# Moving the second product half a unit later and reordering ScalarE's work in a fused top-k attention and gated feed-forward kernel

## The chip, the cores and the metric

The kernel runs on one core of one Trainium2 chip. The metric is device time in microseconds (us) of that core. A core has five engines that are programmed separately: TensorE (PE in the profile, with its weight loads as PEld), VectorE (DVE), ScalarE (ACT), GpSimd (POOL) and SyncE (SP), which here only issues transfers. Each engine works through its own queue of instructions in order and waits on semaphores for the others.

## The reference

There are two blocks in a row. Attention with 8 batches, 8 heads, 576 positions and a head size of 64 keeps the 32 largest scores of each row. Its output, 4608 tokens of 512 values, goes through a feed-forward block whose activation is h cos(h).

```python
scores = scale * np.matmul(q, k.transpose(0, 1, 3, 2))
kth = np.partition(scores, -32, axis=-1)[..., -32:-31]
scores = np.where(scores >= kth, scores, -1000000000.0)
attn = np.exp(scores - np.max(scores, axis=-1, keepdims=True))
attn = attn / (np.sum(attn, axis=-1, keepdims=True) + 1e-09)
x = np.matmul(attn, v)          # then (B,H,S,D) -> (B*S, H*D)
h = x @ w_in                    # 512 -> 2048
out = (h * np.cos(h)) @ w_out   # 2048 -> 512
```

All of it is in float32.

## The kernel before

**Units, blocks and slots.** A unit is one pair of heads for 128 tokens; there are 144. Four units make a block of 128 tokens, of which there are 36. Since 576 is four and a half times 128, every ninth block straddles two batches, and its units have two parts. The main loop makes one pass a unit, called a slot here. In slot i several units are in work at once: unit i (called u) has its 32 largest values searched, the unit before (w) is masked and exponentiated, older ones (x, y, z) are normalised, transposed and multiplied by the values.

**Attention.** `scores` (L213) puts a unit's scores into a PSUM tile `sc` and a shared bank `rim`, and `take_scores` (L228) copies them to `s` on ScalarE. `topk_first` and `topk_round` search on VectorE, which takes most of that engine's time; the middle units are first folded in two halves (`fold`, L235, line 244), and the folded search of w is closed by two small reductions (`merge_first`, `merge_second`, L289 and L296) at the start of the next slot. On ScalarE `bounds` (L309) makes the threshold and the maximum from the merged result, `mask` (L322) pushes everything below the threshold far down, and `exponentials` (L330) makes the weights and their sum `den`. In the next slot VectorE's `reciprocal` (L341, line 343) is the first instruction, so its start marks the start of a slot on that engine. GpSimd's `normalise`, `split` and a transfer then write the weights out in two half-words, a transposing transfer (`transposes`, L367) brings them back as `pT`, and every second slot `values` (L391) multiplies two units at once and `take_values` (L410) copies the result to `xT`.

**The feed-forward block.** It is fed into gaps of the attention. `ff1` (L450) is an eighth of a block's first product, with two eighths to a PSUM bank `mm`; `ff2` (L533) is an eighth of the second product, and all eight of a block add up in one bank `o`. These banks come from the same pool of two. A full bank is put on the list `full`. `take_banks` (L482) empties the listed banks on ScalarE, with `take_first` (`take_g` in the text, L477) for an mm bank and `take_second` (`take_o`, L551) for an o bank. The activation is made for half a block at a time: `reduce_first` and `reduce_second` on GpSimd bring the argument into range, `sines` (L516) runs on ScalarE, and `gate` (L526) multiplies on GpSimd. Sine and exponential need different function tables on ScalarE, so a table load stands where they alternate.

**What sets the order.** The order on each engine is written out by hand: each queue gets its instructions in the order in which `slot` (L666) emits them. Slots 9 to 140 use `slot`; the early and the late ones have functions of their own. `feed(n)` (L575) emits up to n pieces of the feed-forward block. It raises a counter `tick`, spends credit (each slot adds 5 less 0.9 for every unit whose scores it makes, up to 5.3), and takes two pieces of one kind and then two of the other, as far as `can_first` (L560) and `can_second` (L568) allow. `can_second` holds an ff2 back until its gate lies at least two ticks behind. Credit that no piece may use is lost above the cap. A loop at the end of the kernel, the drain, emits two pieces a pass until nothing is left.

In a block that lies in one batch, odd slots make the scores of two units (`made` has two entries) and even slots make none. In a straddling block each slot makes the scores of one unit. Odd slots also run `values` (z is set).

Of the kernel before, what the change touches and what calls it, by code (L numbers as in the profile page):

```python
# [31 lines left out]
def kernel(  # L32
# [16 lines left out]
    NP = H // 2  # L49
# [46 lines left out]
    ff = {"live": 0, "tick": 0, "now": 0, "credit": 0.0, "end": False, "kind": 0, "half": 0, "open": 0}  # L96
# [34 lines left out]
    def decode_second(n):  # L131


        for _ in range(min(n, len(wq["second"]))):
            st, w = wq["second"].popleft()
            wi = w.bitcast(I32)
            nc.vector.tensor_scalar(out=w, in0=w, scalar1=2.0, scalar2=None, op0=ALU.max)
            nc.vector.tensor_scalar(  # L138
                out=wi, in0=wi, scalar1=3, scalar2=None, op0=ALU.logical_shift_left
            )  # L140
            wq["third"].append((st, w))
# [24 lines left out]
    NU = len(units)  # L166
    pairs = {}
    v_tails = []
    for i in range(2 * NP):
        t = consts.tile([P, P], F32, tag=f"v_tail{i}", name=f"v_tail{i}")  # L170
# [79 lines left out]
    for i in range(3):  # L250
        t = consts.tile([P, 2, TOPK, 2], F32, tag=f"top{i}", name=f"top{i}")
# [5 lines left out]
    def topk_first(u, w):  # L257

        u["top"] = tops[u["n"] % len(tops)]
        merges = [merge_first, merge_second] if w and w["folds"] else []  # L260
        if u["folds"]:
            for op in (ALU.max, ALU.min):
                fold(u, op)
                if merges:
                    merges.pop(0)(w)
        else:
            u["rest"] = work.tile([P, 2, S], F32, tag="rest", name="rest", bufs=1)
        for merge in merges:
            merge(w)
        topk_round(u, 0)  # L270

    def topk_round(u, rnd):
        top, rest, lasts = u["top"], u["rest"], TOPK // 8 - 1
        end = TOPK - 1 - 8 * rnd
        at = top[:, :, end : end - 8 if rnd < lasts else None : -1, 0]
        if u["folds"]:
            search(at, rest[:, :, 0:HS], rest[:, :, 0:HS], rnd < lasts)
            if rnd < TOPK // 16:

                low = top[:, :, 1 + 8 * rnd : 9 + 8 * rnd, 1]  # L280
                search(low, rest[:, :, HS:S], rest[:, :, HS:S], rnd < TOPK // 16 - 1)
        else:
            search(at, u["s"] if rnd == 0 else rest, rest, rnd < lasts)
        if rnd == lasts:
            del u["rest"]
# [36 lines left out]
    def mask(u):  # L322

        s, nb = u["s"], u.pop("nb")
        for j in range(2):
            nc.scalar.activation(  # L326
                out=s[:, j], in_=s[:, j], func=AF.Prelu, bias=nb[:, j, 1:2], scale=SCALE, alpha=FAR
            )
# [12 lines left out]
    def reciprocal(u):  # L341
        u["rden"] = small.tile([P, 2], F32, tag="rden", name="rden")
        nc.vector.reciprocal(u["rden"], u.pop("den"))  # L343
# [47 lines left out]
    def values(us):  # L391


        o = room[0]
        for i, u in enumerate(us):
            pT = u.pop("pT")
            for b, _, rows, r0 in u["parts"]:
                st = pairs[b, u["hp"]]
                r = slice(r0, r0 + rows)
                to = slice(i * P + r0, i * P + r0 + rows)  # L400
                for c in range(NT + 1):
                    for j in range(2):
                        d = slice(j * D, (j + 1) * D)
                        if c < NT:
                            lhsT, rhs = st["v"][:, c, d], pT[:, j * (NT + 1) + c, r]
                        else:
                            lhsT, rhs = st["v_tail"][:, d], pT[:, NT, r]
                        nc.tensor.matmul(o[d, to], lhsT, rhs, start=c == 0, stop=c == NT)  # L408
# [16 lines left out]
    for w in widths:  # L425
        blk = {"t0": t0, "w": w, "left": 0, "g": [], "gated": []}
# [23 lines left out]
    def ff1(blk, i):  # L450
        w = blk["w"]
        nf = 256 // w
        part = i % 4
        if part == 0:
            blk["g"].append(ffw.tile([P, 1024], F32, tag="g", name="g", bufs=CHUNKS))
            ff["live"] += 1
        if part % 2 == 0:
            open_bank()
            blk["mm"] = ps.tile([P, 512], F32, tag="mm", name="mm", bufs=2)
        g, mm = blk["g"][-1], blk["mm"]  # L460
        for a in range(nf):
            f = i * nf + a
            at = (part % 2 * nf + a) * w
            for c in range(NC):
                nc.tensor.matmul(  # L465
                    mm[:, at : at + w],
                    w_in[f // FC][:, c, (f % FC) * P : (f % FC + 1) * P],
                    blk["xT"][:, c],
                    start=c == 0,
                    stop=c == NC - 1,  # L470
                )
        if part % 2 == 0:
            return
        ff["open"] -= 1
        full.append((take_first, blk, g, mm, part // 2))
# [6 lines left out]
    def take_banks():  # L482
        while full:
            take, *what = full.popleft()
            take(*what)
# [40 lines left out]
    def gate(n):  # L526
        for _ in range(min(n, len(sined))):
            blk, g, x = sined.popleft()
            eng = nc.vector if ff["end"] else nc.gpsimd
            eng.tensor_tensor(out=g, in0=g, in1=x, op=ALU.mult)  # L530
            blk["gated"].append(ff["tick"])

    def ff2(blk, i, f0):  # L533
        w = blk["w"]
        if f0 == 0:
            open_bank()
            blk["o"] = ps.tile([P, 512], F32, tag="mm", name="o2", bufs=2)
        o = blk["o"]
        per = 1024 // w
        for f in range(f0, f0 + 2):  # L540
            g = blk["g"][f // per]
            at = (f % per) * w + i * P
            nc.tensor.matmul(  # L543
                o, g[:, at : at + P], w_out[f], start=f == 0, stop=f == NF - 1
            )
        if f0 + 2 < NF:
            return
        ff["open"] -= 1
        full.append((take_second, blk, i, o))
# [18 lines left out]
    def can_second():  # L568
        if not second:
            return False  # L570
        blk, i, f = second[0]
        gated = sum(ff["tick"] >= t + 2 for t in blk["gated"])
        return gated * 1024 // blk["w"] >= f + 2 and wq["ready"] >= NC * NF // FC + f + 2

    def feed(n):  # L575

        ff["tick"] += 1
        while n > 0 and ff["credit"] >= 1:
            for kind in (ff["kind"], 1 - ff["kind"]):
                if (can_first, can_second)[kind]():  # L580
                    break
            else:
                return
            if kind == 0:
                ff1(*first.popleft())
            else:
                ff2(*second.popleft())
            if kind != ff["kind"] or ff["half"]:
                ff["kind"], ff["half"] = 1 - kind, 0
            else:  # L590
                ff["half"] = 1
            n, ff["credit"] = n - 1, ff["credit"] - 1
# [73 lines left out]
    def slot(i, u, w, x, y, z):  # L666
        if x:
            reciprocal(x)
        if u:
            topk_first(u, w)  # L670
            decode_second(2)
        if u:
            topk_round(u, 1)
            topk_round(u, 2)
            topk_round(u, 3)
        if z:
            values(z)
        made = scored.get(i, [])
        if not made or not z:
            feed(1)  # L680
        for m in made:
            scores(m)


        late = z and len(made) == 2
        if not made:
            take_banks()
        if w:
            bounds(w)
            mask(w)  # L690
        if w and late:
            exponentials(w)
        take_banks()
        if z:
            take_values(z)
        take_scores(units[i + 1])
        if w and not late:
            exponentials(w)
        for load, b, hp in at_slot.get(i, []):
            load(b, hp)  # L700
        load_weights(2)
        if y:
            transposes(y)
        gate(1)
        if x:
            normalise(x)
            split(x)
            write_halves(x)
        feed(2)
        take_banks()  # L710
        decode_third()
        decode_first(2)
        reduce_first()
        reduce_second()
        feed(1 if late else 3)
        if i % 2:
            sines(1)
        elif i < EARLY + 8 or i > LAST - 2:
            sines(2)
# [51 lines left out]
    for i in range(NU + 1):  # L771
# [6 lines left out]
        z = units[i - 5 : i - 3] if i % 2 and EARLY <= i - 5 < LAST else None  # L778
# [53 lines left out]
```

## Time and profile before

The time is 1538.96 us, the median of three runs (1538.32 to 1544.69); the profiled execution spans 1537.8 us.

| engine | busy us | share of the span |
|---|---|---|
| TensorE, matmuls | 1419.5 | 92% |
| TensorE, weight loads (beside the matmuls) | 1018.8 | 66% |
| VectorE | 1416.3 | 92% |
| ScalarE | 1158.8 | 75% |
| GpSimd | 1105.3 | 72% |

The chain of work that ended last is TensorE for 80% of the span; line 465 (first product) and line 543 (second product) make 30% each, line 408 (values) 10%, line 220 (scores) 9%. The costliest groups are VectorE's search for maxima (L304, 681.6 us), the first product (L465, 554.5 us of matmuls), the second product (L543, 529.4 us) and VectorE's replacing of found maxima (L307, 495.0 us). The granted clock of TensorE is 1.00 in most of the span, lower in the first 250 us and at some places later.

In the views below, a wait is the time for which an engine stood still before an instruction, and the name after the arrow is what ended it. Idle time of an engine that is not the bound costs nothing, so a wait counts only where the engine that waits is short of time.

### The profile page before, as it was taken

Reading aid. Unit: us, or ns where it says so; the run is one execution under the profiler, and the core shown is the slowest. Engines: PE = TensorE matmul, PEld = TensorE weight load, DVE = VectorE, ACT = ScalarE, POOL = GpSimd, SP = SyncE. Lnnn points to the kernel's source line nnn. Section 1 sums busy time; section 2 is a strip of 40 time slices with the busy share of each in tenths; the row PEclk is TensorE's granted clock in tenths of the full one; section 3 lists DMA queues with packets and bytes.
Section 4 is the critical chain, followed back from the end, with each engine's and each line's share of the span. In section 5 each row is a group of like instructions: output and inputs, shape, how many; then the busy total and the mean of one; then the engine's idle time right before and its main releaser. Section 6 shows DMA issues by size and latency. Waiting matters only on the chain.

```text
span 1537.8 us, 30197 instructions
## 1 busy us (share of the span) xinstructions
PE 1419.5 (92%) x10360; PEld 1018.8 (66%) x10360; DVE 1416.3 (92%) x4689; ACT 1158.8 (75%) x2326; POOL 1105.3 (72%) x838
## 2 busy tenths in 40 slices
PE   4577789999999999999999999999999999999999
PEld 2365366777677766777777766777777766777675
DVE  7989998999999998999999998999999998999821
ACT  7888776777777777777777777777777776777741
POOL 4777966777777776777777776777777776777610
PEclk6687899999999999999999999999999999999999
DMA  8422465545654456545564455545555455545300
GB/s 270 139 85 71 113 192 132 145 133 169 162 147 132 132 155 164 163 131 148 167 162 137 133 146 162 158 130 154 170 163 129 133 136 143 133 130 132 99 8 14
DMA packets 371753, 212.20 MB, mean 138 GB/s; under 512 B 321296, under 2 KB 337936, under 8 KB 371600
## 3 DMA queue, kind: packets, MB, share of 16 engines
q1 hardware_dynamic: 366192, 200.63, 47.3%
q10 hardware_dynamic: 5408, 9.65, 1.8%
q8 instruction: 81, 1.33, 0.4%
q14 instruction: 72, 0.59, 0.1%
HBM read 45.09 MB, written 87.29 MB: 86 GB/s over the span
## 4 chain that ended last, share of the span: by engine, by line
PE 80%; ACT 8%; DVE 4%; POOL 3%; DMA 2%; SPq 1%; issue 1%; ACTq 0%; POOLq 0%; DVEq 0%
PE mm L465 30%; PE o L543 30%; PE rim L408 10%; PE sc L220 7%; PE rim L220 2%; ACT g L478 2%; DVE top L304 2%; ACT s L334 1%; DVE rest L307 1%; DMA pT<-rows 1%; ACT s L326 1%; DVE w_out L138 1%; POOL s L348 1%; ACT st L127 1%; ACT s L230 1%
## 5 line engine op out<-in xcount | busy, mean ns | idle before, releaser
L304 DVE MAX8 top<-rest 128x8 f32<-128x288 f32 (+1 forms) x1656 | 681.6, 460 | 0.0
L465 PEld LDWEIGHTS mm<-xT,w_in 128*128 128x128 f32 x4608 | 538.3, 194 | 80.1 <-ACT g L478 41.0
L465 PE MATMUL mm<-xT,w_in 128*128 128x128 f32 x4608 | 554.5, 279 | 32.8 <-ACT g L478 32.8
L543 PE MATMUL o<-w_out,g 128*128 128x512 f32 x1152 | 529.4, 602 | 12.7 <-POOL g L530 6.8
L307 DVE MATCH_REPLACE8 rest<-top,rest 128x288 f32<-128x288 f32 (+1 forms) x1104 | 495.0, 456 | 0.0
L543 PEld LDWEIGHTS o<-w_out,g 128*128 128x128 f32 x1152 | 209.5, 192 | 228.9 <-issue 208.8
L360 POOL COPY halves<-s 128x2304 uint16<-128x2304 uint16 x132 | 277.7, 2103 | 17.1 <-DMA rows<-halves 9.2
L348 POOL TENSOR_SCALAR s<-s,rden 128x576 f32<-128x576 f32 x288 | 212.8, 751 | 52.1 <-DVE rden L343 52.1
L530 POOL TENSOR_TENSOR g<-g,x 128x1024 f32<-128x1024 f32 x68 | 160.6, 2362 | 99.3 <-ACT x L523 86.8
L334 ACT ACTIVATE s<-s,nd 128x576 f32<-128x576 f32 x288 | 220.0, 765 | 0.8
L244 DVE TENSOR_TENSOR rest<-sc,s 128x576 f32<-128x576 f32 x264 | 198.6, 753 | 8.0 <-ACT s L231 2.3
L326 ACT ACTIVATE s<-s,nb 128x576 f32<-128x576 f32 x288 | 205.4, 760 | 0.0
L504 POOL TENSOR_SCALAR x<-g 128x1024 f32<-128x1024 f32 x68 | 71.1, 1046 | 168.7 <-ACT g L478 168.7
L408 PEld LDWEIGHTS rim<-pT,v 128*64 128x64 f32 x2560 | 134.8, 141 | 71.6 <-ACT g L478 23.5
L408 PE MATMUL rim<-pT,v 128*64 128x128 f32 (+1 forms) x2560 | 162.9, 272 | 15.7 <-ACT pT L389 13.3
L478 ACT ACTIVATE g<-mm 128x512 f32<-128x512 f32 x144 | 84.5, 588 | 122.3 <-PE mm L465 122.3
L513 POOL TENSOR_TENSOR x<-g,x 128x1024 f32<-128x1024 f32 x68 | 161.1, 2370 | 5.7
L220 PE MATMUL sc<-k,q 64*128 64x448 f32 (+1 forms) x640 | 150.7, 585 | 14.9 <-DMA k<-in_k_dram 8.9
L314 ACT ACTIVATE nb<-top 128x4 f32<-128x4 f32 x144 | 29.4, 204 | 141.2 <-DVE top L297 129.0
L230 ACT COPY s<-sc 128x896 f32<-128x896 f32 x144 | 128.9, 895 | 6.6 <-PE sc L220 6.2
L220 PEld LDWEIGHTS rim<-k,q 64*128 64x128 f32 (+1 forms) x640 | 57.2, 182 | 58.9 <-issue 53.9
L523 ACT ACT_TABLE_LOAD x68 | 87.2, 1283 | 1.6 <-ACT ob L553 0.4
(55 smaller groups left out, 1244.1 us busy)
## 6 DMA issues: line engine op xcount, KB each, us to landing
rows<-halves SPq DMA_DIRECT2D x132, 576.0 KB, 2.9
out_dram<-ob ACTq DMA_DIRECT2D x36, 256.0 KB, 3.4
q<-in_q_dram SPq DMA_DIRECT2D x31, 288.0 KB, 3.2
st<-in_moe_w_in_dram SPq DMA_DIRECT2D x16, 512.0 KB, 5.5
v<-in_v_dram SPq DMA_DIRECT2D x32, 256.0 KB, 3.2
st<-in_moe_w_out_dram SPq DMA_DIRECT2D x16, 512.0 KB, 3.5
k<-in_k_dram SPq DMA_DIRECT2D x31, 144.0 KB, 3.3
k<-in_k_dram SPq DMA_DIRECT2D x32, 128.0 KB, 3.5
```

What stands on the lines that cost most here:

```text
L220: nc.tensor.matmul(to[r0 : r0 + rows, j, 0 : k1 - k0], st["q"][d, q0 : q0 + rows], st["k"][d, k0:k1], start=True, stop=True,)
L244: nc.vector.tensor_tensor(out=u["rest"][:, :, i * HS : (i + 1) * HS], in0=sc[:, :, 0:HS], in1=s[:, :, HS:S], op=op,)
L304: nc.vector.max(to[:, j], src[:, j])
L307: nc.vector.match_replace(rest[:, j], to[:, j], src[:, j], NEG)
L326: nc.scalar.activation(out=s[:, j], in_=s[:, j], func=AF.Prelu, bias=nb[:, j, 1:2], scale=SCALE, alpha=FAR)
L334: nc.scalar.activation(out=s[:, j], in_=s[:, j], func=AF.Exp, bias=nd[:, j : j + 1], scale=1.0, accum_out=den[:, j : j + 1],)
L348: nc.gpsimd.tensor_scalar(out=s[:, j], in0=s[:, j], scalar1=rden[:, j : j + 1], scalar2=1.0, op0=ALU.mult, op1=ALU.mult,)
L360: nc.gpsimd.tensor_copy(out=halves, in_=s.rearrange("p (k h) -> p h k", h=2))
L408: nc.tensor.matmul(o[d, to], lhsT, rhs, start=c == 0, stop=c == NT)
L465: nc.tensor.matmul(mm[:, at : at + w], w_in[f // FC][:, c, (f % FC) * P : (f % FC + 1) * P], blk["xT"][:, c], start=c == 0, stop=c == NC - 1,)
L513: nc.gpsimd.tensor_tensor(out=x, in0=g, in1=x, op=ALU.subtract)
L543: nc.tensor.matmul(o, g[:, at : at + P], w_out[f], start=f == 0, stop=f == NF - 1)
```

## The change

It does three things. Second products wait for three ticks after their gate instead of two, from slot 20 to slot 138; its purpose is that no three first products stand in a row while a second product holds one of the two banks. Exponentials go ahead of `take_scores` and `take_values` wherever the slot makes scores, not only where it makes two. And full banks are emptied after the mask, where slots before emptied them ahead of the bounds; slots with `values` empty them right behind it, at the head of ScalarE's part of the slot.

```diff
@@ can_second @@
         blk, i, f = second[0]
-        gated = sum(ff["tick"] >= t + 2 for t in blk["gated"])
+
+        lag = 3 if 5 * NP < ff["now"] < NU - NP else 2
+        gated = sum(ff["tick"] >= t + lag for t in blk["gated"])
@@ slot @@
         if z:
             values(z)
         made = scored.get(i, [])
-        if not made or not z:
+        if z:
+            take_banks()
+        else:
             feed(1)
         for m in made:
             scores(m)
 
 
-        late = z and len(made) == 2
-        if not made:
-            take_banks()
+        late = len(made) > 0
         if w:
             bounds(w)
             mask(w)
+        take_banks()
         if w and late:
             exponentials(w)
-        take_banks()
         if z:
             take_values(z)
         take_scores(units[i + 1])
@@ slot @@
-        feed(1 if late else 3)
+        feed(1 if len(made) == 2 else 3)
```

In the loop over slots 9 to 140 every odd slot makes the scores of at least one unit, so a slot with z set and no scores, which would now call no first `feed(1)`, does not occur.

## The prediction

> **What bounds the kernel now.** I read the busy shares of the page first, then busy time block by block, then the waits, then the order of time. The first fence is the page's busy row; the second holds two stretches: length, then busy us of PE, PEld, DVE, ACT, POOL, the granted clock, DMA share.
>
> ```profile
> PE 1419.5 (92%) x10360; PEld 1018.8 (66%) x10360; DVE 1416.3 (92%) x4689; ACT 1158.8 (75%) x2326; POOL 1105.3 (72%) x838
> ```
>
> ```profile
> 641.80:680.10 38.30, 37.62 (x272) 27.17 (x272) 37.65 (x131) 30.37 (x62) 29.69 (x23) 1.00 0.46 129
> ...
> 910.00:955.20 45.20, 40.64 (x299) 28.16 (x297) 39.91 (x141) 30.50 (x61) 31.81 (x25) 0.96 0.54 154
> ```
>
> The reader sees two engines at 92%, both with less than a microsecond free in a regular block (four slots), and a block that straddles two batches taking 45 us instead of 38. Neither engine alone is the bound: each waits for ScalarE (ACT), which is only 75% busy. So order on ACT matters, not work. The waits from 300 to 1300 us (total, times, longest) say which:
>
> ```profile
> ACT g L478 <- PE mm L465: 79.4, 51, 3.3
> ...
> PE mm L465 <- ACT g L478: 28.0, 31, 2.9
> ...
> DVE rden L343 <- ACT den L339: 27.9, 31, 4.1
> ```
>
> The order of time shows how. First a regular stretch, then the straddling stretch (start, duration; in brackets the idle time before it and its releaser):
>
> ```profile
> 641.12 0.60 ACT L478 ACTIVATE g<-mm 128x512 f32<-128x512 f32 x1 [1.86 <-PE mm L465]
> ...
> 641.77 3.84 PE L465 MATMUL mm<-xT,w_in 128*128 128x128 f32 x32 [0.69 <-ACT g L478]
> ...
> 660.77 0.60 ACT L553 ACTIVATE ob<-o 128x512 f32<-128x512 f32 x1 [0.38 <-PE o L543]
> ...
> 661.80 0.20 ACT L314 ACTIVATE nb<-top 128x4 f32<-128x4 f32 x1 [0.44 <-ACT ob L553]
> ...
> 668.28 0.17 DVE L343 RECIPROCAL rden<-den 128x2 f32<-128x2 f32 x1 [0.47 <-ACT den L339]
> ```
>
> ```profile
> 565.75 0.58 ACT L478 ACTIVATE g<-mm 128x512 f32<-128x512 f32 x1
> ...
> 566.38 2.05 PE L465 MATMUL mm<-xT,w_in 128*128 128x128 f32 x16 [2.93 <-ACT g L478]
> ...
> 573.71 0.37 ACT L414 COPY xT<-rim 128x256 f32<-128x256 f32 x1 [3.42 <-PE rim L220]
> ...
> 589.13 0.17 DVE L343 RECIPROCAL rden<-den 128x2 f32<-128x2 f32 x1 [2.54 <-ACT den L339]
> ```
>
> Regular: PE stands 0.69 us once a block, because two mm groups follow each other while o holds the other bank, and ACT must empty the first. DVE stands about 0.4 us once a block, because the o bank's emptying (waiting for PE) sat ahead of the bounds: 661.80 instead of 660.07, where the merge ended. Straddling: PE waits 2.93 us for an emptying queued behind two exponentials, and exponentials are queued behind a take_values that waits for a late PE.
>
> **What the Trainium skill says.** "TensorE: Matmul & The Clock Gate", section "Architectural detail", has ScalarE and VectorE as strict FIFO queues; the waits above, passed on by ACT instructions that need nothing from PE, agree. "Perfetto Trace Analysis", "Optimizing Tensor Performance", wants independent matmul groups to rotate through PSUM banks so that the emptying of one lies beside the next group; here o keeps one of two banks for most of a block, and the 0.69 us is the cost. "ScalarE: Activation LUTs", "What ACT_TABLE_LOAD costs", gives about 1283 ns a load; the trace has 1283. The first page, "HAM oscillation", warns that PE idle of over some 3 us brings the half clock; after a 2.93 us stand at 917.22 the sixteen matmuls took 3.53 us instead of 2.05, and the clock of that stretch was 0.96.
>
> **Prices from the trace.** One first-product half (ff1) 1.88 us, start to start, at 1465.14 to 1467.02. One second-product half (ff2) 1.72 us (the last eight, 13.75 us). values 2.34 (648.97 to 651.31). Two scores 2.15 (651.31 to 653.46). Bank emptying 0.6. bounds and mask 2.05, mask to the end of an exponential pair with den about 2.0, plus 1.28 of table load in even slots; take_scores 1.25. A DVE slot with no stall 9.50 (187.32 to 244.32 is six slots of it).
>
> **The lag.** Following credit, tick and kind through the loop reproduces the PE order of the trace, and gives for a steady block after the change: odd slot: values, two scores, ff2 ff2, ff1; even slot: ff1, ff2 ff2, ff1 ff1. Between any two mm groups now lie two ff2, 3.44 us. The 0.69 us stand goes. A half's lag also means six calls less by slot 30 (the loop spends no credit on ff2 that are not due): they end up in the drain, where the last run of ff2 is 12 long instead of 8. That is 6 x 1.72 = 10.3 us more after the last slot. The order has two spots, slots 20 and 28, in which six ff1 come in a row.
>
> **Emptying behind the mask.** Even slot, from its DVE start: merge at 1.87, bounds and mask to 3.95, take_g to 4.5 (its ff1 ended at about 1.9), take_scores 5.8, load 7.1, exponentials and den 9.0. DVE needs den at 9.46: hidden, by 0.4 to 0.5. PE's next mm group starts after two ff2, at 5.3, and its bank is free at 4.5: hidden by 0.8. Queued behind take_g on ACT are take_scores and the exponentials; DVE waits for these at the next slot. Cost 0, and DVE's 0.4 us goes.
>
> **Emptying at the head of odd slots.** take_g waits for the second ff1 of the pair, that is for the start of values, about 0.4 us before the DVE slot starts. It ends at 0.3; the merge is at 1.87. Hidden while PE is less than 1.6 us late. Behind it are bounds, mask, exponentials and take_scores, for which DVE waits.
>
> **Regular block.** DVE 4 x 9.50 = 38.0; PE's busy 37.6 fits under it. Before it is 38.34. There are 23.5 such blocks from slot 33 to 139: 23.5 x 0.33 = 7.8 us.
>
> **Exponentials first.** It acts in straddling slots alone. Even ones: bounds, mask, take_g, load, exponentials, take_scores end at 9.3 after the slot's start, against 9.5: just hidden. Odd ones: the exponentials no longer wait for take_values, so the 2.54 and 1.15 us of DVE go. With ff2 between the ff1 pairs the 2.93 us of PE goes too, and so does the slow clock after it. By DVE's slot starts the three straddling stretches of eight slots (556.88 to 639.18, 907.69 to 991.28, 1259.80 to 1344.28) are 6.3, 7.6 and 8.5 us above eight times 9.50: 22.4. I leave 1 us each for the pT transposes, which are queued behind the loads of q and k (a 0.51 us wait of that kind is there now): 19.4 gained.
>
> **Transition.** Slots 20 to 27 are now 5.7 us above 9.50 a slot. 2.3 of this, scores that come late at slot 20, stays. New: at slot 21 the head take_g waits for the sixth ff1, some 3 us past the merge, and take_scores comes about 1.3 us late; around slots 28 to 31 PE stands some 6 us for the mask and then for the exponentials, the head take_g is about 4 us late, DVE loses 2.0 and, with two sines ahead of the bounds, 1.6 more. With 0.3 for den at slot 21 the sum is 7.5. That is 1.8 more than before. The six ff2 taken out of these slots keep PE from being the bound there. Between slot 27 and slot 33 the old order loses about 1.3 that also goes.
>
> **Sum.** Before, slot 20 to 140 took 244.32 to 1421.48 = 1177.2 us. 120 x 9.50 = 1140, plus 7.5 and 3: 1150.5, a gain of 26.7, which is the sum of the parts (7.8 + 19.4 - 1.8 + 1.3). Drain: 10.3 more, less 1.3 for stands there that the order removes (0.83 at 1492.08 and 0.65 at 1474.41, most of it). Net 26.7 - 9.0 = 17.7. 1538.96 - 17.7 = 1521.3.
>
> **Rivals.** First, gain eaten: in even slots take_g between mask and exponentials fills the 0.4 us margin, regular blocks stay at 38.3 (7.8 lost), and straddling stretches give 10 instead of 19.4: 26.7 - 17.2 - 9.0 = 0.5, or 1538.5. For it: the margins are a few tenths on a path of nine; against: the merge releases ACT 1.7 us sooner than now. Second, a new wait: PE runs late, so the head take_g holds the bounds of odd slots and DVE loses 0.5 a slot, two a block. 23.5 x 1.0 = 23.5 on 38.0, so regular gives -15.7; with 10 from the straddling stretches, -1.8 + 1.3 and drain -9.0: -15.2, or 1554. For it: PE has only 0.4 us a block to catch up. Against: the wait must exceed 1.6 us first, and a late PE falls back on 37.6, below today's block. Third, a better one: stalls of the transition are absorbed (5 of 7.5) and pT costs nothing (3): 1513.
>
> **How the numbers follow.** My forecast 0.60; the better one 0.14; gain eaten 0.15; new wait 0.11. Unknown sizes: transition stalls, 2.5 to 14; pT, 0 to 6; drain, 8 to 12. These put the forecast between 1512 and 1532. Gain eaten is taken in, the new wait only to its near side: 1508 to 1544. Faster by over 0.5% is below 1531.3: both good cases less a twentieth, 0.73 with a part of the eaten one. Same 0.16, slower 0.11.
>
> **What would show it.** Right: a regular block of 38.0 us between DVE reciprocals, no 0.69 before mm, sets of two ff1 and two ff2 in turn; straddling stretches near 77 us for eight slots; a last run of ff2 half as long again, some 20.6 us; the granted clock 1.00 at 910 to 1310. Wrong: reciprocals waiting for den or the folds for take_scores once a block, PE waiting for take_g in even slots, or ACT's g waiting for PE at the head of odd slots past the merge. The forecast fails most easily if the transition loses more than 14 us.

## The result

The changed kernel takes 1523.12 us, the median of four runs (1521.09 to 1523.88); the kernel before 1539.54 us, also of four (1538.32 to 1544.69). The ratio is 0.9885, with a 95% interval of 0.986 to 0.991: 1.15% faster. The forecast was 1521.3 us.

The page of the changed kernel shows almost the same work (its busy row, then the shares of the chain of work that ended last; the third line is that chain before the change).

```profile
PE 1417.3 (93%) x10360; PEld 1020.5 (67%) x10360; DVE 1416.0 (93%) x4690; ACT 1149.2 (76%) x2322; POOL 1102.9 (72%) x837
...
DVE 74%; PE 12%; ACT 6%; issue 3%; POOL 2%; DMA 2%; SPq 1%; DVEq 0%; ACTq 0%; POOLq 0%
...
PE 80%; ACT 8%; DVE 4%; POOL 3%; DMA 2%; SPq 1%; issue 1%; ACTq 0%; POOLq 0%; DVEq 0%
```

PE's and DVE's busy times differ by 2.2 and 0.3 us from those of before. What has changed is the chain: it now runs through VectorE for 74% of the span, where it ran through TensorE for 80%. The same can be read in a table by stretches, answering to the one of before (length, then busy us of PE, PEld, DVE, ACT, POOL, the granted clock, DMA share and GB/s).

```profile
641.80:679.90 38.10, 38.10 (x282) 27.83 (x278) 37.88 (x133) 30.47 (x62) 29.95 (x23) 1.00 0.49 132
...
910.00:955.20 45.20, 44.95 (x367) 32.78 (x366) 44.91 (x156) 35.64 (x72) 36.80 (x27) 1.00 0.64 175
```

In the straddling stretch VectorE was busy 39.91 of 45.20 us before, and is busy 44.91 now. The clock there, 0.96 before, is 1.00. PE's 38.10 of 38.10 doesn't say that PE is full: the Trainium skill ("Perfetto Trace Analysis", "Identifying the Most-Contended Engine") warns that the matmul row is a poor measure, since matmuls are pipelined; the weight loads of the same stretch are busy for 27.83 us, about as before (27.17). Yet PE has little to spare: at the prediction's prices its work in a regular block (eight ff1, eight ff2, two values, two pairs of scores) is 37.8 us, an estimate, of the 38.04 that the block takes.

The waits from 300 to 1300 us (total, times, longest) answer to the three lines shown of before; a fourth of before stands last.

```profile
ACT nb L314 <- DVE top L297: 180.2, 105, 4.3
...
ACT g L478 <- PE mm L465: 9.3, 11, 1.6
...
PE mm L465 <- ACT g L478: 1.1, 2, 0.9
...
ACT nb L314 <- DVE top L297: 90.9, 54, 2.3
```

PE's 28.0 us for an emptied bank have become 1.1, ACT's 79.4 for a filled one 9.3, and DVE's wait for `den`, 27.9 us, is no longer in the list. In their place ACT waits for DVE's merge (L297), 180.2 us where it was 90.9: the engine between the two now stands still because VectorE is the last.

The order of time in a regular block (start, duration, idle time before it and its releaser in brackets):

```profile
651.22 3.60 PE L543 MATMUL o<-w_out,g 128*128 128x512 f32 x8
652.42 0.57 ACT L478 ACTIVATE g<-mm 128x512 f32<-128x512 f32 x1
...
654.65 3.73 PE L465 MATMUL mm<-xT,w_in 128*128 128x128 f32 x32
...
657.03 0.30 ACT L339 ACTIVATE den<-den,eps 128x2 f32<-128x2 f32 x1
658.09 0.15 DVE L343 RECIPROCAL rden<-den 128x2 f32<-128x2 f32 x1
...
658.42 0.60 ACT L478 ACTIVATE g<-mm 128x512 f32<-128x512 f32 x1 [1.10 <-PE mm L465]
...
659.97 0.21 ACT L314 ACTIVATE nb<-top 128x4 f32<-128x4 f32 x1 [0.94 <-DVE top L297]
```

Two second products (L543) lie between two groups of first products. The bank that the group at 654.65 takes was emptied at 652.42 to 652.99, 1.7 us ahead. `den` is ready at 657.33, here 0.76 us before DVE's next slot begins. And the emptying at the head of the odd slot (658.42) waits for PE, yet ends before the merge that ACT waits for anyway. Before, the first products (L465) had a bracket of 0.69 and the reciprocal (L343) one of 0.47; here neither has any, and the 0.94 of ACT's bounds (L314) is a wait for the engine that sets the end.

Where the time went, by the starts of DVE's reciprocals (L343):

| stretch | before, us | after, us | difference |
|---|---|---|---|
| start to slot 20 | 244.3 | 245.2 | +0.9 |
| slot 20 to slot 140 | 1177.2 | 1145.6 | -31.6 |
| - a regular block, mean of seven | 38.36 | 38.04 | |
| - eight slots around each straddling block | 82.3, 83.6, 84.5 | 76.1, 76.1, 76.1 | |
| - slots 20 to 33, above 9.505 us a slot | 5.9 | 4.0 | |
| slot 140 to the end | 116.3 | 131.1 | +14.8 |

So the loop gave 31.6 us, and nearly half of that was given back behind it. The 0.9 us at the start is no effect of the change as far as is shown: the kernel with the lag alone has the same code as the kernel before up to slot 20, and begins slot 20 at 245.1.

### The profile page after: what moved, and what is told of

It reads as the page before. It is cut to its first block, busy times and chain, and to the rows that moved or that the text cites. A ratio compares the mean times of both kernels' runs of the same rounds, so it can differ in the third digit from the quotient of the medians.

```text
span 1521.9 us, 30207 instructions
## 1 busy us (share of the span) xinstructions
PE 1417.3 (93%) x10360; PEld 1020.5 (67%) x10360; DVE 1416.0 (93%) x4690; ACT 1149.2 (76%) x2322; POOL 1102.9 (72%) x837
## 4 chain that ended last, share of the span: by engine, by line
DVE 74%; PE 12%; ACT 6%; issue 3%; POOL 2%; DMA 2%; SPq 1%; DVEq 0%; ACTq 0%; POOLq 0%
DVE top L304 33%; DVE rest L307 27%; DVE rest L244 11%; PE o L543 5%; PE mm L465 4%; PE rim L408 2%; ACT s L334 1%; DVE top L292 1%; ACT s L326 1%; DVE top L297 1%; DVE w_out L138 1%; PE sc L220 1%; DMA pT<-rows 1%; DVE rden L343 1%; ACT st L127 1%
## 5 line engine op out<-in xcount | busy, mean ns | idle before, releaser
L465 PEld LDWEIGHTS mm<-xT,w_in 128*128 128x128 f32 x4608 | 536.3, 193 | 83.4 <-ACT g L478 39.8
L465 PE MATMUL mm<-xT,w_in 128*128 128x128 f32 x4608 | 546.9, 277 | 7.4 <-ACT g L478 3.4
L543 PE MATMUL o<-w_out,g 128*128 128x512 f32 x1152 | 532.1, 605 | 11.3 <-POOL g L530 5.6
L543 PEld LDWEIGHTS o<-w_out,g 128*128 128x128 f32 x1152 | 209.3, 192 | 232.4 <-issue 210.4
L314 ACT ACTIVATE nb<-top 128x4 f32<-128x4 f32 x144 | 29.6, 206 | 230.2 <-DVE top L297 229.6
L230 ACT COPY s<-sc 128x896 f32<-128x896 f32 x144 | 129.0, 896 | 3.3 <-PE sc L220 3.3
L523 ACT ACTIVATE x<-x,halfpi 128x1024 f32<-128x1024 f32 x72 | 82.5, 1149 | 6.9 <-DVE x L499 6.1
```

The costliest lines, as they stand in the source:

```text
L465: nc.tensor.matmul(mm[:, at : at + w], w_in[f // FC][:, c, (f % FC) * P : (f % FC + 1) * P], blk["xT"][:, c], start=c == 0, stop=c == NC - 1,)
L523: nc.scalar.activation(out=x, in_=x, func=AF.Sin, bias=halfpi, scale=scale)
L543: nc.tensor.matmul(o, g[:, at : at + P], w_out[f], start=f == 0, stop=f == NF - 1)
```

## The experiments

Two theories stood against each other on the loop. A: PE's order does it, that is, the lag alone. B: ScalarE's order does it, that is, the emptying behind the mask and the exponentials first. My own text had credited DVE's 0.4 us a block and the straddling waits to B. Ratios below are against the kernel before on the same chip (1541.2 us in the first four runs, 1541.5 in the last four, 1539.5 in the result above). The changed kernel was not run again beside them, so differences from its 1523.12 us carry up to 2 us of doubt.

**The lag alone.** The kernel before, with one line changed.

```diff
-        gated = sum(ff["tick"] >= t + 2 for t in blk["gated"])
+        lag = 3 if 5 * NP < ff["now"] < NU - NP else 2
+        gated = sum(ff["tick"] >= t + lag for t in blk["gated"])
```

> The lag of three ticks alone; ScalarE's order stays as before the change. Theory A (the order of PE does the work: two second-product halves between any two mm groups): a regular block falls to 38.0 us and the 0.69 us stand before mm goes; in straddling blocks the 2.93 us of PE goes, while den still comes late behind take_values in odd slots, 1 to 2 us a straddling block: 1523 to 1530 us, about 1527. Rival B (ScalarE's order does the work): the emptying ahead of the bounds still waits for PE in even slots, DVE still loses 0.4 us a block and 6 to 8 us a straddling stretch, and the drain is 10 us longer: 1540 to 1549 us.

Measured: 1527.91 us, ratio 0.992 (0.990 to 0.9939). A regular block takes 38.06 us, the straddling stretches 76.0: all of the steady gain. The waits show what is left to the other edits:

```profile
ACT nb L314 <- DVE top L297: 172.9, 94, 4.5
...
ACT g L478 <- PE mm L465: 27.0, 46, 2.7
```

ACT still waits for PE with an emptying ahead of the bounds, 46 times, but PE's new order fills the bank early enough that DVE loses nothing by it. In the loop only slots 20 to 33 differ: 10.3 us above 9.505 a slot, where the whole change has 4.0. The order of time shows the start of it:

```profile
252.19 0.60 ACT L478 ACTIVATE g<-mm 128x512 f32<-128x512 f32 x1 [1.55 <-PE mm L465]
...
259.15 0.17 DVE L343 RECIPROCAL rden<-den 128x2 f32<-128x2 f32 x1 [1.55 <-ACT den L339]
...
259.58 5.47 PE L465 MATMUL mm<-xT,w_in 128*128 128x128 f32 x32 [2.91 <-ACT g L478]
```

An emptying ahead of the bounds waits 1.55 us for PE, and DVE waits as long for `den`. Then PE stands 2.91 us for a bank, and its next 32 matmuls take 5.47 us instead of 3.84 (the last section says why).

**ScalarE's new order alone.** The changed kernel with the old lag.

```diff
-        lag = 3 if 5 * NP < ff["now"] < NU - NP else 2
+        lag = 2
```

> ScalarE's new order without the lag (two ticks as before). Theory A: four first products still stand in a row once a block, and their bank is now emptied only behind the mask, some 2 us later than before: the stand before mm grows from 0.69 to about 2.7 us, a regular block from 38.34 to about 40.3, and the time to 1565 to 1595 us. Rival B: DVE's wait for den goes, a regular block falls to about 38.0, and without the longer drain the time is 1510 to 1520 us.

Measured: 1595.21 us, ratio 1.0353 (1.0326 to 1.038), the upper end of A's range, with a regular block of 41.05 us on average. With the old PE order the second of two first-product groups in a row needs its bank at once, and the emptying is now queued behind the mask:

```profile
DVE rden L343 <- ACT den L339: 65.5, 25, 3.3
...
PE mm L465 <- ACT g L478: 52.2, 28, 2.2
...
ACT xT L414 <- PE rim L220: 51.8, 27, 2.6
```

PE stands 1.9 us each time (52.2/28) and falls behind; `take_values` (L414) then waits for PE, and DVE for a late `den` (65.5/25 = 2.6 us). Not all of this is waiting. After 17 such stands, from slot 20 to the end, TensorE's granted clock fell to 0.50 for 3.41 us. Regular blocks with such a stretch take 41.4 to 41.5 us, those without 39.9, close to the 40.3 expected; 17 times 1.6 us makes about 27 us, an estimate, of the 54. B is refuted as the source of the gain: without the lag its edits cost 54 us.

**The exponentials-first edit undone, the rest kept.**

```diff
-        late = len(made) > 0
+        late = z and len(made) == 2
```

> The change without its exponentials-first part: late is again only where two scores are made with values. It acts in straddling blocks alone. Theory A: with PE in step, take_values and take_scores hardly delay the exponentials, so each of the three straddling stretches loses at most 2 us: 1523 to 1529 us. Rival B: the exponentials carry the gain of the straddling stretches, and 4 to 7 us come back in each of three: 1535 to 1544 us.

Measured: 1523.11 us, ratio 0.9887 (0.9866 to 0.9908), straddling stretches 76.0 each, all as with the whole change. With PE on time, DVE's wait for `den` is in neither kernel's list of waits from 300 to 1300 us: no gain of this edit shows beside the other two.

**The emptying as before, the rest kept.** Before the change only slots without scores emptied banks ahead of the bounds; odd slots of a regular block did so behind the exponentials, slots of a straddling block right behind the mask. This run puts the calls back, but as the exponentials now go first, in straddling blocks the emptying comes behind them.

```diff
         made = scored.get(i, [])
-        if z:
-            take_banks()
-        else:
+        if not made or not z:
             feed(1)
...
         late = len(made) > 0
+        if not made:
+            take_banks()
         if w:
             bounds(w)
             mask(w)
-        take_banks()
         if w and late:
             exponentials(w)
+        take_banks()
```

> Lag and exponentials first, but banks emptied where they were: ahead of the bounds in slots without scores, else behind the exponentials. Theory A: in regular blocks the emptying ahead of the bounds costs some 0.6 us of ScalarE that the 0.5 us margin of den nearly covers, 0 to 0.2 us a block; in straddling even slots PE waits for the emptying behind the exponentials, about 2 us twice a block: 1523 to 1534 us. Rival B: emptying ahead of the bounds is what holds DVE; its 0.4 us a block stays, 10 us in all, and with the longer drain the time is 1532 to 1540 us.

Measured: 1534.94 us, ratio 0.9961 (0.9949 to 0.9972), just above A's range and inside B's. The blocks decide against B: regular ones lose nothing (38.05), slots 20 to 33 lose what they lose with the lag alone (9.4), and each straddling stretch loses another 3 to 4 us (79.1 to 80.0). There the emptying stands behind the exponentials, and PE stands 2.35 us for it, in two of the three with a slow group as well:

```profile
565.21 5.34 PE L465 MATMUL mm<-xT,w_in 128*128 128x128 f32 x32 [2.35 <-ACT g L478]
...
911.54 3.84 PE L465 MATMUL mm<-xT,w_in 128*128 128x128 f32 x32 [2.35 <-ACT g L478]
```

So exponentials first is no gain in itself. Added to the lag alone it costs 7.0 us (1534.94 - 1527.91), and this cost goes away when banks are emptied between mask and exponentials.

The remaining four runs concern the 14.8 us behind the loop and the transition at slot 20. From slot 140 on, the trace of the changed kernel has these two stretches (slots 140 to 144, then the drain; columns as above):

```profile
1390.79:1458.76 67.97, 61.73 (x427) 45.89 (x426) 42.42 (x116) 44.05 (x92) 30.94 (x25) 0.92 0.18 48
1458.76:1521.90 63.14, 59.37 (x281) 37.98 (x279) 10.66 (x10) 9.85 (x13) 0.00 (x0) 1.00 0.04 13
```

and the kernel before has these:

```profile
1421.48:1483.94 62.46, 58.22 (x434) 41.85 (x433) 41.16 (x115) 41.28 (x89) 31.10 (x26) 1.00 0.22 62
1483.94:1537.80 53.86, 49.33 (x257) 33.48 (x255) 10.57 (x10) 11.25 (x14) 0.00 (x0) 1.00 0.04 15
```

The second stretch grew by 9.3 us, the six more second products that I had forecast. The first grew by 5.5 us, and its clock fell to 0.92. In order of time, PE in the changed kernel, and last the final run of second products before the change:

```profile
1408.56 0.66 PE L382 MATMUL tp<-ident,s 128*128 128x128 f32 x4 [2.31 <-POOL s L348]
1410.51 0.45 PE L382 MATMUL rim<-ident,s 128*128 128x128 f32 x1 [1.29 <-ACT s L231]
...
1426.76 0.45 PE L382 MATMUL rim<-ident,s 128*128 128x128 f32 x1 [2.33 <-ACT s L231]
...
1497.36 20.77 PE L543 MATMUL o<-w_out,g 128*128 128x512 f32 x48
...
1520.21 13.90 PE L543 MATMUL o<-w_out,g 128*128 128x512 f32 x32
```

and ACT between them, in the same kernel:

```profile
1406.58 1.28 ACT L523 ACT_TABLE_LOAD   x1
1407.87 1.15 ACT L523 ACTIVATE x<-x,halfpi 128x1024 f32<-128x1024 f32 x1
...
1409.98 0.38 ACT L231 COPY s<-rim 128x256 f32<-128x256 f32 x1
```

In the last slots a table load and a sine are emitted ahead of `take_scores`, and PE waits for that copy of the shared bank `rim`. Before the change, too, a sine stood ahead of the first of these copies (1436.79), but PE did not wait; the one ahead of the second (1423.11) is due there only with the lag. The stand of 2.31 us is a wait for GpSimd. After the stands of 2.31 and 1.29 us the next sixteen first-product matmuls, at 1411.60, take 3.62 us; undisturbed sixteens took 2.05. The granted clock was 0.50 for 6.83 us there (from 1409.62) and for 3.41 more after the stand of 2.33. If work at half the clock loses half its time, that is up to 5.1 of the 5.5 us, an estimate.

**The sines of the last slots behind `take_scores`.** The changed kernel, with one line of `last_slot` moved.

```diff
         take_banks()
-        sines(1)
         if z:
             values(z)
...
         if i + 1 < NU:
             take_scores(units[i + 1])
+        sines(1)
```

> The change, and in the last slots (last_slot) the sines are emitted behind take_scores instead of ahead of it. Theory A: of the 14.8 us that slots 140 to the end have gained, 9 are six second-product halves that moved to the drain, and the other 5.5 (68.0 us for slots 140 to 144 instead of 62.5) come from PE standing for a take_scores that is queued behind a table load and a sine (2.3 and 1.3 us), and the low clock after that (0.92 in that stretch). Without the sine in front the stands go and the clock stays up: 3.5 to 6 us less, 1517 to 1520 us. Rival: those slots are longer because PE has more and other work there, and the stands move elsewhere: within 1.5 us of the change, 1521.5 to 1524.5 us.

Measured: 1518.3 us, ratio 0.9848 (0.9832 to 0.9864). The loop is unchanged (1145.5), slot 140 to the end takes 125.7 instead of 131.1. The stands for the scores are gone; a later one is 0.74, as this trace's PE shows:

```profile
1408.82 0.66 PE L382 MATMUL tp<-ident,s 128*128 128x128 f32 x4 [2.32 <-POOL s L348]
...
1410.41 3.32 PE L465 MATMUL mm<-xT,w_in 128*128 128x128 f32 x16
...
1425.69 1.09 PE L408 MATMUL rim<-pT,v 128*64 128x128 f32 x16 [0.74 <-ACT pT L389]
```

The 2.32 us stand alone was enough for one stretch of half clock: the sixteen matmuls at 1410.41 took 3.32 us. So not all of the 5.4 us is the edit's own. The run with the lag from slot 12, below, has the old place of the sines and also one such stretch in its tail, which takes 128.3 us; against that the edit is worth 2.6.

**A lag of four.**

```diff
-        lag = 3 if 5 * NP < ff["now"] < NU - NP else 2
+        lag = 4 if 5 * NP < ff["now"] < NU - NP else 2
```

> The change with a lag of four ticks instead of three. The order in regular blocks keeps its pattern of two and two, with second products two halves further behind (eight instead of six), so the last run of ff2 has 14 halves. Theory A: the lag costs what it moves into the drain, 2 x 1.72 = 3.4 us more, and the regular block stays at 38.0: 1525.5 to 1528 us. Rival: second products that run further behind leave room in PE's stretch from slot 20 to 140, or the pattern, not the amount, makes the drain: within 1 us of the change, 1522 to 1524 us.

Measured: 1528.9 us, ratio 0.9918 (0.9902 to 0.9934), 5.8 us over the changed kernel and 0.9 over the expectation's upper end. Regular blocks stay at 38.05; slot 140 to the end takes 134.1, 3.0 more, for two more halves in the drain (2 x 1.72 = 3.4). Slots 20 to 33 take 1.4 more. The rest is two slots of 11.06 and 10.96 us at 402.39 and 422.86. Ahead of the first, PE stood for a transposing transfer:

```profile
396.28 1.98 PE L408 MATMUL rim<-pT,v 128*64 128x128 f32 x16 [2.93 <-DMA pT<-rows]
```

It ran its sixteen matmuls in 1.98 instead of 1.09 us, and exponentials queued behind `take_values` came late. The transfer was late because two issued before it, at 381.59 and 384.87, took 9.01 and 6.90 us to land, where their counterparts in the changed kernel took 5.38 and 3.19. Why these did stays open. Three of the six runs of this kernel, at 1527.7 to 1527.9, lie inside A's range; whether they were spared that delay is not known.

**The lag from slot 12.** In the changed kernel the lag sets in at slot 20 and puts six first products in a row there.

```diff
-        lag = 3 if 5 * NP < ff["now"] < NU - NP else 2
+        lag = 3 if 3 * NP < ff["now"] < NU - NP else 2
```

> The change with the lag from slot 12 on instead of slot 20, so that one run of six first products leaves slots 19 to 21 and the first products are spread over slots 15 to 18, where PE has idle time. Theory A: the 4.0 us that slots 20 to 33 take above 9.5 a slot come from the runs of six in the transition; about half of it goes: 1520 to 1522 us. Rival: they come from the backlog of the straddling block before (slots 15 to 18), and stay: 1522.5 to 1524.5 us.

Measured: 1517.97 us, ratio 0.9846 (0.983 to 0.9863). The expectation had 1520 to 1522. Slots 20 to 33 take 0.1 us above 9.505 a slot, slots 16 and 17 1.2 in return, and slot 140 begins at 1386.97 instead of 1390.79: 3.8 us earlier. Slot 140 to the end took 128.3 instead of 131.1 with the same code there, so that a part of the 5.1 us is no merit of the edit. That difference goes with the clock: from slot 140 on it was 0.50 for 10.24 us in the changed kernel's trace and for 3.41 here.

**Both.** The lag from slot 12, and the sines behind `take_scores`.

> Both edits together: sines behind take_scores in the last slots and the lag from slot 12. Theory A: the gains add, 1515 to 1519 us. Rival: neither acts, 1521.5 to 1524.5 us.

Measured: 1513.94 us, ratio 0.982 (0.9803 to 0.9837). The two edits' gains over the changed kernel are 5.2 and 4.8; together they give 9.2, 1.1 us below the expected range. It is the fastest of all versions here, faster than before and after.

## Why the prediction was right

The forecast of 1521.3 us was 1.8 us below the measured time. The direction holds, and so does the mechanism of the lag. What the forecast said of ScalarE does not: that its order is what matters, and that the emptying behind the mask and the exponentials first bring part of the steady gain. The lag alone brought all of it. That the sum came so near is partly luck, since the loop was 4.9 us better than forecast and the rest 5.8 worse.

- **The regular block.** Forecast 38.0, measured 38.04, from 38.36; PE's 0.69 and DVE's 0.4 us are gone. Right in size per block. The attribution of the 0.4 to the emptying behind the mask was wrong: the lag alone has 38.06. Two terms of the old loop were also off by about 1 us and cancel: the 23.5 regular blocks overlap the stretches of eight slots (slots 33 to 139 less three times eight are 20.5 blocks, 6.8 us), and between slots 27 and 33 the old trace loses 0.3 us, not 1.3. The gain of 26.7 came from the measured 1177.2 us and rests on neither.
- **The straddling stretches.** Forecast near 77 us for eight slots, measured 76.1. The 1 us each that I had left for the `pT` transposes cost nothing: PE did wait for them (0.98 us at 564.56), but values had room. I credited the exponentials first with removing DVE's waits; the runs show that PE's order did, and that the edit is worth nothing here. The clock from 300 to 1300 us is 1.00, as forecast.
- **The transition.** Forecast 7.5 us, measured 4.0. Slot 20's own stall and the late scores at slot 22 came as said (DVE slots of 11.43 and 11.66 us). The stall of 3.6 at slots 28 to 31 did not come. I had PE standing about 6 us for banks; in PE's order of time there it stood 2.15 (for `take_values`, not for a bank) and 0.94:

```profile
321.79 6.96 PE L465 MATMUL mm<-xT,w_in 128*128 128x128 f32 x60 [2.15 <-ACT xT L414]
...
329.69 3.84 PE L465 MATMUL mm<-xT,w_in 128*128 128x128 f32 x32 [0.94 <-ACT g L478]
```

  The six in a row are there, but no second product was open in slot 28, so that both banks served first products. I had counted one as held. All slots from 23 to 139 start without a stall on VectorE.
- **The loop's sum.** Forecast 1150.5, measured 1145.6: 3.5 from the transition and 2.8 from `pT`, less 0.04 a block (0.9) and 0.5 in other slots.
- **Behind the loop.** Forecast +9.0, measured +14.8. The term for the drain was right (+9.3; the last run of second products is x48 and 20.77 us, after x32 and 13.90). What I had left out is the stretch ahead of the drain, slots 140 to 144, 5.5 us longer, up to 5.1 of it by the half clock after PE's stands. The move of one line got back 4.8 us in the median and 5.4 by the traces, 2.6 where the clock was alike.
- **The rivals.** The gain was not eaten: `den` comes 0.76 us early where I had 0.4 to 0.5. The new wait did not come: the head of odd slots waits for PE, but ends before the merge. The better case, 1513, came nearer on the loop (1142.5 by its terms) and left out the tail in the same way.

What ScalarE's new order brings over the lag alone lies in slots 20 to 33, where the lag alone loses 6.3 us more (10.3 to 4.0): PE is late there, and an emptying ahead of the bounds passes that on to VectorE. One stretch of half clock, up to 1.7 us by the same estimate, is part of the 6.3. Whether the new order is still worth anything when the lag starts at slot 12 was not tried.

## What to carry to other kernels

When a long accumulation holds one of two banks, set the order so that short groups never follow each other while it is open; here the emptying engine's order then did not matter in regular blocks (one order of it still cost 3 to 4 us in each straddling stretch), and with the old order on the matmul engine the better-looking order on the emptying engine cost 3.5%. Work that a lag takes out of the loop comes back at the end, where nothing hides it: count it there, and look through the tail's own code for instructions whose order assumed the old timing. When two edits seem to remove the same wait, run each alone before crediting either.

## What was not expected of the hardware

A matmul group after a stand can run at about half speed, and the length of the stand alone does not decide it. In the kernel with the old lag the same stand of 2.24 us comes before the same 32 matmuls, once without effect and once with it:

```profile
415.17 3.84 PE L465 MATMUL mm<-xT,w_in 128*128 128x128 f32 x32 [2.24 <-ACT g L478]
...
455.06 5.46 PE L465 MATMUL mm<-xT,w_in 128*128 128x128 f32 x32 [2.24 <-ACT g L478]
```

The traces show what does decide. From slot 20 to the last matmul, the granted clock in the ten traces is 1.00 or 0.50. It was 0.50 in 38 stretches, 33 of 3.41 us and five of 6.83. Within one trace their starts lie whole multiples of 3.41 us apart; in the kernel with the old lag, 332.94, 373.90 and 455.82 are 12 and 24 such steps from each other. Lay a grid of these steps over each trace and count how much of a step PE is busy by the profile. Of the 38 stretches, 37 follow a step in which it was busy for 15 to 42%, one a step with 51%. No step with 42% or less was followed by the full clock; the lowest that was had 43%. So a stand that falls into one step brings half clock for the next, and one of this length that the edge of a step cuts in two does not. In the kernel with the sines moved, the stand of 2.32 us lies within the first of these steps (columns as in the tables by stretches):

```profile
1406.45:1409.86 3.41, 1.02 (x8) 0.74 (x8) 3.41 (x14) 3.38 (x6) 1.47 (x2) 1.00 0.37 94
1409.86:1413.27 3.41, 3.41 (x19) 3.41 (x17) 3.34 (x9) 2.00 (x4) 2.57 (x2) 0.50 0.49 110
```

With both edits the same stand, 1404.81 to 1407.12, is cut by an edge at 1406.18 (counted back from that trace's half clock at 1511.99, after the last matmul), and the sixteen matmuls behind it took 1.95 us. The grid starts at a different point in every trace, so an order cannot choose which of its stands are hit; it can only avoid them. The Trainium skill ("TensorE: Matmul & The Clock Gate", "HAM oscillation") puts the limit at idle gaps of about 3.4 us; gaps of 2.1 to 2.9 us were enough here where they fell into one step.

So a stand of 2 us on this engine can cost 1.6 us on top of itself. It also explains most of a spread: with the same code from slot 140 on, that part took 131.1 us in the changed kernel, 129.0 with the exponentials edit undone and 128.3 with the lag from slot 12, with 10.24, 6.83 and 3.41 us of half clock.
